# One core, attention and a soft mixture of experts: first-layer weights in longer runs and partly on another queue, a 512-wide second layer, and a new order of stages

## The chip, the core and the metric

The kernel runs on one core of one Trainium2 chip. The time is the device time of an execution in microseconds (us). Before the change, 8 executions took 182.0 us at the median, 181.5 to 182.68. One further execution was recorded by the hardware profiler; every view below is of that one.

## What is computed

The inputs are `q`, `k`, `v` of shape (8 batches, 8 heads, 576 positions, 64), `phi` (512 x 32), `w1` (8 experts, 512 x 1024) and `w2` (8 experts, 1024 x 512), all f32. Attention has a window of 32 positions, plain for heads 0 to 3 and with dilation 4 for heads 4 to 7. Its output, as 4,608 tokens of 512 features, goes through a soft mixture of experts with 4 slots an expert:

```python
scores = where(mask[h], q @ k.T / 8, -1e9);  x = softmax(scores) @ v      # x: (4608, 512)
logits = x @ phi
d = softmax over tokens of logits;   slot_input = (d.T @ x).reshape(8, 4, 512)
slot_out[e] = relu(slot_input[e] @ w1[e]) @ w2[e]
c = softmax over slots of logits;    out = c @ slot_out                   # (4608, 512)
```

Every expert's slots depend on all tokens, so the first layer can't start before attention has ended for the last batch, and no output can be stored before the second layer is done.

## The kernel before, in words

**A planner orders the work.** The program builds a list of operations, each with an engine, an assumed duration, a priority and its buffers. `Sched.run` then walks through time: of the operations that are ready on an engine at about the same time, the one with the lowest priority number goes first. Each engine executes its operations in the order so found, with a semaphore wait where an operation depends on another engine. The priority of a stage of half `i` is `i * PERIOD + OFFS[stage]`. It decides the order on an engine, not a start time.

**Attention** goes by 16 halves: batch `i // 2`, heads 0 to 3 or 4 to 7. For each, GpSimd (POOL) issues the loads of k, q and v (`load_half`, L328), which cast f32 to bf16 on the way into one of four staging buffers. VectorE (DVE) transposes them in 32 x 32 blocks (L455, L461), TensorE (PE) makes the scores with the mask added by an identity matmul (L475, L482, L492, L499), ScalarE (ACT) takes the exponential (L514), PE transposes v (L536) and ACT copies it out (L542), PE multiplies by v (L569, L593), and DVE divides (L576, L580, L601, L604). After the two halves of a batch, PE transposes x (L620, L626), ACT copies (L636, L639, L643), PE makes the logits (L659), ACT their exponential (L667), PE transposes that (L682), ACT copies it (L688), and PE and DVE add to the slot sums (L700, L708). In L626 and L700 a chunk of 128 features is a contiguous range.

**Loads** are all issued by POOL in one written order: the three loads of a half, then as many w1 pieces as `W_AFTER` says (two after half 1, one after most others), and after half 15 the last w1 piece and all of w2. A w1 piece (`w1_piece`, L338) is 256 rows, 1 MB of f32: partition p gets rows p and p + 128, two runs of 4 KB. A w2 piece (L345) is 1 MB in runs of 8 KB. The last two experts' w2 comes in slabs of half the columns (`w2_slab`, L352, runs of 1 KB), so that the left half of the output can be made while the right half's weights still load. Experts 5 to 7 of w2 use the space of the staging buffers. Some mask and identity tiles are built at the start on POOL (L381 to L411, selects at L388) and DVE (memsets from L400 to L424, L397, L402); POOL's loads of halves 2 and later stand behind its mask selects. `phi` is loaded by SP (L432) and converted by DVE (L437).

**The tail.** The first layer is 64 matmuls of 512 columns (L765) with a relu on ACT (L773) and a transpose (L783, L788). The second layer (`l2`, L801) is made for the left 256 columns and the right 256 columns apart, each in a PSUM bank of its own, 32 x 256 a matmul; ACT copies each result (L818). The output is 36 tiles of 128 tokens (L836), scaled on ACT (L845) and DVE (L848) in turn, and stored by SP (L856). The first three groups of 512 tokens (`NA = 3`) are stored in half rows, left and then right; groups 3 to 8 in full rows, two tiles (512 KB) a store.

## Time and profile before

| | |
|---|---|
| median of 8 executions | 182.0 us |
| profiled execution | 181.82 us |
| its span, first to last instruction | 180.0 us |
| PE, DVE, ACT, POOL busy | 126.2, 113.5, 104.3, 52.8 us |
| read from HBM, written | 61.93 MB, 9.44 MB |
| queue fed by POOL, queue fed by SP | 30.94 MB, 9.50 MB as written at the destination |
| k, q, v load: size, issue to landing | 288 KB each as written, 19.8 to 20.2 us |

In the views, "PEld" is TensorE's loading of weights, "SPq" and "POOLq" are instructions that issue transfers, and "a <- b" after an idle time names what ended it. "GB/s" counts the bytes that the transfers write: a load that casts f32 to bf16 reads twice as much. The "DMA share" is the mean busy share of 16 transfer engines by the durations of their packets; overlapping packets bring it over 1. "PEclk" is the granted share of TensorE's clock.

### The profile page before, as it was taken

The page shows a single profiled execution, that of the slowest core. Times are in us where ns is not written, and L with a number is a line of the kernel's source. Part 1 is how long each engine was busy: PE and PEld are TensorE (multiplying, and loading weights), DVE is VectorE, ACT ScalarE, POOL GpSimd, SP SyncE. Part 2 cuts the span into 40 slices and gives each one's busy share as a digit, 9 for nine tenths or more (in the row PEclk, how much of TensorE's full clock was granted, in tenths as well). Part 3 has the DMA queues.
Part 4 walks back from the last instruction along what each step waited for, and adds up shares of the span by engine and source line. Part 5 has one row for each costly group of instructions (what it writes and reads, how often), then busy time and mean ns, then how long its engine had stood idle before and what let it go on. Part 6 is the DMA issues. An engine that isn't in the chain of part 4 may idle for free.

```text
span 180.0 us, 5369 instructions
## 1 busy us (share of the span) xinstructions
PE 126.2 (70%) x2268; PEld 89.4 (50%) x2268; DVE 113.5 (63%) x211; ACT 104.3 (58%) x167; POOL 52.8 (29%) x99
## 2 busy tenths in 40 slices
PE   0027795989699799797898897795659766898000
PEld 0004474767467577476676675584434554442000
DVE  6898382957899798998879797835020103299200
ACT  0007366579778788869889788684324103399000
POOL 7679922223235244245860000740000000000000
PEclk9999996599999999999999999997556998799755
DMA  5999999999999999999999999999999999979998
GB/s 68 196 209 213 209 211 212 212 209 210 210 212 213 209 211 210 211 211 210 211 209 213 209 213 212 217 211 213 216 211 215 198 197 159 328 265 388 404 406 318
DMA packets 22727, 40.78 MB, mean 227 GB/s; under 512 B 2224, under 2 KB 9392, under 8 KB 22704
## 3 DMA queue, kind: packets, MB, share of 16 engines
q0 software_dynamic: 17184, 30.94, 93.0%
q1 hardware_dynamic: 5520, 9.50, 14.2%
q8 instruction: 18, 0.29, 0.6%
q14 instruction: 5, 0.04, 0.1%
HBM read 61.93 MB, written 9.44 MB: 396 GB/s over the span
## 4 chain that ended last, share of the span: by engine, by line
DMA 44%; PE 20%; DVE 15%; ACT 8%; issue 3%; POOL 1%; DVEq 0%; ACTq 0%
DMA ar<-in_v_dram 25%; DMA ar<-in_moe_w_dram 19%; PE ps L475 5%; ACT ar L514 5%; DVE ar L455 4%; DVE ar L848 4%; PE ps L836 3%; PE ps L801 2%; PE ps L482 2%; PE ps L536 2%; PE ps L569 2%; DVE ar L580 2%; DVE ar L415 2%; ACT ar L636 1%; PE ps L659 1%
## 5 line engine op out<-in xcount | busy, mean ns | idle before, releaser
L455 DVE STREAM_TRANSPOSE ar<-ar 128x576 uint32<-128x576 uint32 x40 | 48.1, 1244 | 2.4 <-DMA ar<-in_k_dram 1.8
L514 ACT ACTIVATE ar<-ps 128x1152 bf16<-128x1152 f32 (+1 forms) x32 | 38.1, 1192 | 13.9 <-PE ps L499 8.6
L475 PE MATMUL ps<-ar 128*128 128x320 bf16 (+1 forms) x128 | 24.1, 314 | 18.8 <-DVE ar L455 12.6
L542 ACT ACTIVATE ar<-ps 128x768 bf16<-128x768 bf16 x32 | 25.6, 831 | 2.8 <-PE ps L536 2.7
L580 DVE TENSOR_TENSOR ar<-ps,fs 96x768 bf16<-96x768 f32 (+1 forms) x32 | 26.3, 823 | 1.3
L475 PEld LDWEIGHTS ps<-ar 128*128 128x128 bf16 x128 | 11.0, 102 | 23.4 <-POOL ar L388 12.6
L848 DVE TENSOR_SCALAR ar<-ps,fs 128x256 f32<-128x256 f32 (+1 forms) x24 | 12.9, 611 | 12.7 <-PE ps L836 12.7
L569 PE MATMUL ps<-ar 128*128 128x65 bf16 x320 | 15.3, 199 | 6.6 <-ACT ar L514 3.3
L536 PE MATMUL ps<-ar 128*128 128x128 bf16 x192 | 17.8, 239 | 1.4 <-issue 0.5
L569 PEld LDWEIGHTS ps<-ar 128*128 128x128 bf16 x320 | 12.6, 101 | 9.0 <-ACT ar L514 5.2
L576 DVE RECIPROCAL fs<-ps 96x12 f32<-96x12 f32 (+1 forms) x32 | 6.1, 192 | 16.8 <-PE ps L569 16.7
L536 PEld LDWEIGHTS ps<-ar 128*128 128x128 bf16 x192 | 13.9, 122 | 3.2 <-issue 1.6
L328 POOL DMA_DIRECT2D ar<-in_k_dram x16 | 9.3, 582 | 20.7 <-DVE ar L455 11.6
L639 ACT ACTIVATE ar<-ps 128x1024 bf16<-128x1024 bf16 x8 | 8.2, 1022 | 7.6 <-PE ps L626 7.6
L345 POOL DMA_DIRECT2D ar<-in_moe_w_dram x12 | 6.4, 586 | 20.6 <-DVE fs L601 20.6
L328 POOL DMA_DIRECT2D ar<-in_v_dram x16 | 8.8, 551 | 12.2 <-DVE ar L455 7.5
L836 PE MATMUL ps<-ar 128*128 128x256 bf16 (+1 forms) x48 | 11.1, 356 | 1.8 <-ACT ar L818 1.0
L845 ACT ACTIVATE ar<-ps,fs 128x256 f32<-128x256 f32 (+1 forms) x24 | 11.5, 618 | 1.2 <-PE ps L836 1.2
L328 POOL DMA_DIRECT2D ar<-in_q_dram x16 | 8.8, 549 | 10.0 <-DVE fs L576 4.9
L338 POOL DMA_DIRECT2D ar<-in_moe_w_dram x16 | 11.7, 737 | 0.0
L659 PE MATMUL ps<-ar 128*128 128x288 bf16 x64 | 10.3, 306 | 1.9 <-ACT ar L643 1.9
L801 PE MATMUL ps<-ar 128*32 128x256 bf16 x128 | 8.8, 280 | 2.7 <-DMA ar<-in_moe_w_dram 2.3
(65 smaller groups left out, 179.3 us busy)
## 6 DMA issues: line engine op xcount, KB each, us to landing
ar<-in_moe_w_dram POOLq DMA_DIRECT2D x30, 512.0 KB, 26.3
out_dram<-ar SPq DMA_DIRECT2D x12, 512.0 KB, 5.0
ar<-in_k_dram POOLq DMA_DIRECT2D x16, 288.0 KB, 19.9
ar<-in_q_dram POOLq DMA_DIRECT2D x16, 288.0 KB, 19.8
ar<-in_v_dram POOLq DMA_DIRECT2D x16, 288.0 KB, 20.2
out_dram<-ar SPq DMA_DIRECT2D x12, 256.0 KB, 3.5
ar<-in_moe_w_dram POOLq DMA_DIRECT2D x4, 256.0 KB, 34.9
fs<-in_moe_phi_dram SPq DMA_DIRECT2D x1, 64.0 KB, 2.0
```

Source lines behind the costliest of these rows:

```text
L328: return pool.dma_start(a(o_stg + (s * 3 + j) * 1152, [[1, 1152]]), src[b, 4 * dl:4 * dl + 4].rearrange("h (p t) d -> (h p) (t d)", p=32))
L455: return dve.transpose(au(o_dst, [[1, 18], [18, 32]]), au(src, [[32, 18], [1, 32]]))
L475: pe.matmul(pf(h, 0, [[1, W]]), a(o_id, [[1, 128]]), a(msk, [[1, W]]), start=True, stop=False)
L514: eo = op(ACT, lambda P=P, W=W: act.activation(a(P, [[W, 4], [1, W]]), AP(ps, 0, [[4096, 128], [512, 4], [1, W]]), ACTF.Exp, scale=SCALE), ...
L536: last = pe.transpose(pb(bank.idx, bb * 256 + par * 32, [[64, 4], [1, 32]]), src, a(o_id, [[1, 128]]))
L542: op(ACT, lambda t=t, bank=bank: act.activation(a(o_vb[vs] + 3 * t * VBK, [[66, 12], [2, 32], [1, 2]]), pb(bank.idx, 0, [[64, 12], [1, 32] ...
L569: last = pe.matmul(pf(bank.idx + x, 65 * t, [[1, 65]]), w, a(VB + t * VBK + 66 * h, [[1, 65]]), start=True, stop=True)
L580: op(DVE, lambda hp=hp, bank=bank: dve.tensor_tensor(a(ox + 128 * hp, [[64, 2], [256, NT], [1, 64]], 0, rows), pf(bank.idx, 0, [[512, 2], ...
L659: last = pe.matmul(pf(bank.idx, 0, [[1, 288]]), a(o_phis + 128 * c, [[1, 128]]), a(o_xt[xt] + 576 * c + 288 * g, [[1, 288]]), start=(c == ...
L801: last = pe.matmul(pf(sobank[s].idx, 0, [[1, 256]], 32 * j, 32), a(o_htz + 1024 * g + 128 * c + 32 * j, [[1, 32]]), a(w2off(e) + DM * c + ...
L836: op(PE, lambda: pe.matmul(pf(bank.idx, 0, [[1, cw]]), a(o_et + 512 * G + j, [[4, 128]]), a(o_so + c0, [[1, cw]]), start=True, stop=True), ...
L848: op(DVE, lambda: dve.tensor_scalar(dst, src(), sca, None, op0=AluOp.mult), dvet(cw, True), prio + .1, reads=[bank, b_rinv], writes=wr, na ...
```

## The change

- The rows 0, 2, 4, ... 254 of the first expert's w1 (512 KB of f32) are loaded by SP as its first instruction, uncast, into space that w2 of expert 4 uses later; ACT converts them with a copy as its first instruction. POOL's first w1 piece loads the other 128 rows alone.
- In a w1 piece, partition p now gets rows 2p and 2p + 1: one run of 8 KB. So that the first layer's chunks fit, x is cut into chunks of even and odd features: `phi` is loaded in that order (runs of 256 bytes instead of 128), and L620, L626 and L700 read x with a step of two features.
- The second layer of experts 0 to 5 is made 512 columns wide into a bank of its own. Partitions 0 to 63 (slots of experts 0, 1, 4, 5) are copied by ACT to their place, partitions 64 to 127 by DVE to f32 scratch. Experts 6 and 7 are still made by halves, and a DVE add replaces ACT's copy of each half.
- Groups 3 to 8 are stored with one 1 MB store each, after four tiles.
- `PERIOD` and all stage offsets are other numbers. Together with the new parts they give another order on PE, ACT and DVE; POOL's order of loads is the same. At the start, DVE now does the first k transpose ahead of L397 and L402, and POOL has the k load of half 2 ahead of the last two mask selects. Towards the end of attention, ACT copies the v of half 15 (L542) right after the last exponential; before, copies of half 14's x (L636, L639, L643, L688) stood between.

```diff
-PERIOD = 6.9
+PERIOD = 13.0
-OFFS = dict(T=0.0, SC=0.6, EX=1.2, MK=2.2, TB=1.0, VE=1.8, PV=4.0, RC=4.4, NM=4.6,
-            XT=6.6, XE=7.0, LG=8.0, EXL=8.5, ET=9.0, EE=9.4, SI=9.8, SA=10.2)
+OFFS = dict(T=11.1, SC=0.6, EX=1.0, MK=13.2, TB=-8.2, VE=-1.3, PV=-27.6, RC=-28.0, NM=-27.1,
+            XT=-13.0, XE=1.8, LG=-37.3, EXL=16.9, ET=26.7, EE=14.5, SI=23.9, SA=8.8)
...
-    def w1_piece(e, hf):
+    def w1_piece(e, hf, r0=0, n=2):
         def fn():
             return pool.dma_start(
-                a(o_w1 + e * 4096 + hf * 2048, [[1024, 2], [1, 1024]]),
-                moe_w1[e, 256 * hf:256 * hf + 256, :].rearrange("(c p) f -> p c f", p=128))
+                a(o_w1 + e * 4096 + hf * 2048 + 1024 * r0, [[1, 1024 * n]]),
+                moe_w1[e, 256 * hf:256 * hf + 256, :].rearrange("(p two) f -> p (two f)", two=2)
+                [:, 1024 * r0:1024 * (r0 + n)])
...
-        wq += [w1_piece(e, 0), w1_piece(e, 1)]
+        wq += [w1_piece(e, 0, 1, 1) if e == 0 else w1_piece(e, 0), w1_piece(e, 1)]
...
+    op(SP, lambda: spq.dma_start(
+        af(w2off(4), [[1, 1024]]),
+        moe_w1[0, 0:256, :].rearrange("(p two) f -> p two f", two=2)[:, 0, :]), .1, -200.0,
+       kind="dma", nbytes=1 << 19, sem=sem("s_w1f"), writes=b_w2[4], name="w1f")
+    op(ACT, lambda: act.activation(a(o_w1, [[1, 1024]]), af(w2off(4), [[1, 1024]]), ACTF.Copy),
+       1.1, -200.0, reads=b_w2[4], writes=[b_w1[0]], name="w1c")
...
-        f(o_phst, [[32, 4], [1, 32]]),
-        moe_phi.rearrange("(c p) s -> p c s", p=128)), .1, 20.0,
+        f(o_phst, [[64, 2], [1, 64]]),
+        moe_phi.rearrange("(hf p two) s -> p hf (two s)", hf=2, two=2)), .1, 20.0,
...
-                                            a(ox + 256 * t + 128 * x, [[1, 128]], 0, 96),
+                                            a(ox + 256 * t + x, [[2, 128]], 0, 96),
...
-                                            a(ox + 256 * t + 128 * par, [[1, 128]]),
+                                            a(ox + 256 * t + par, [[2, 128]]),
...
-                                     a(o + 256 * t + 128 * par, [[1, 128]], 0, rows),
+                                     a(o + 256 * t + par, [[2, 128]], 0, rows),
...
+    l2((0, 1, 2, 3), 0, 0, 512)
+    l2((4, 5), 0, 0, 512)
+    op(ACT, lambda: act.activation(a(o_so, [[1, 512]], 0, 64), pf(sobank[0].idx, 0, [[1, 512]], 0, 64),
+                                   ACTF.Copy), actt(512), T1 + 10, reads=[sobank[0]], writes=b_so,
+       name="SOx")
+    op(DVE, lambda: dve.tensor_copy(af(o_sx, [[1, 512]], 64, 64), pf(sobank[0].idx, 0, [[1, 512]], 64, 64)),
+       dvet(512, True), T1 + 10, reads=[sobank[0]], writes=[b_sx, b_p[2]], name="SOy")
+    for x in (1, 2):
+        l2((6,), x, 256 * x - 256, 256, bufs=[b_w2[6][x - 1]])
+        for y in range(2):
+            l2((7,), x, 256 * x - 256, 256, range(4 * y, 4 * y + 4), [b_w2h[y][x - 1]])
+        op(DVE, lambda x=x: dve.tensor_tensor(
+            a(o_so + 256 * x - 256, [[1, 256]], 64, 64), pf(sobank[x].idx, 0, [[1, 256]], 64, 64),
+            af(o_sx + 512 * x - 512, [[1, 256]], 64, 64), AluOp.add), dvet(256, True),
+           T1 + 10 + 20 * x, reads=[sobank[x], b_sx], writes=[b_so[x - 1]], name=f"SO{x - 1}")
...
     for G in range(NA, 9):
-        for x in range(0, 4, 2):
-            for j in (x, x + 1):
-                out_tile(G, j, 0, 512, T2 + 10 + G + .25 * x)
-            store(G, 0, 512, T2 + 10 + G + .25 * x + .2, x, 2)
+        for j in range(4):
+            out_tile(G, j, 0, 512, T2 + 10 + G)
+        store(G, 0, 512, T2 + 10 + G + .5)
```

## The prediction

> **What bounds the kernel now.** I read the page's second part first, the span in 40 slices, because it shows at a glance whether an engine or the transfers are never idle.
>
> ```profile
> DMA  5999999999999999999999999999999999979998
> GB/s 68 196 209 213 209 211 212 212 209 210 210 212 213 209 211 210 211 211 210 211 209 213 209 213 212 217 211 213 216 211 215 198 197 159 328 265 388 404 406 318
> ...
> HBM read 61.93 MB, written 9.44 MB: 396 GB/s over the span
> ...
> DMA 44%; PE 20%; DVE 15%; ACT 8%; issue 3%; POOL 1%; DVEq 0%; ACTq 0%
> ```
>
> The DMA row is 9 everywhere but in the first slice, in one near 158 us and at the end. The GB/s row counts bytes written: loads read f32 and write bf16, so 211 GB/s written is 422 read. At that rate the reads take 61.93/0.422 = 147 us and the stores at 406 another 23 us: 170 of 180 us. So the transfers set the time, and only their holes or their rate can change it. Next I read the busy time of the engines by stretches, to size holes and rates (columns: PE, PEld, DVE, ACT, POOL busy, clock, DMA share, GB/s).
>
> ```profile
> 0.00:1.80 1.80, 0.00 (x0) 0.00 (x0) 0.65 (x2) 0.00 (x0) 0.76 (x5) 1.00 0.00 0
> 1.80:2.40 0.60, 0.00 (x0) 0.00 (x0) 0.60 (x1) 0.00 (x0) 0.60 (x2) 1.00 0.69 109
> 2.40:3.40 1.00, 0.00 (x0) 0.00 (x0) 0.72 (x2) 0.00 (x0) 1.00 (x3) 1.00 0.69 48
> 14.00:104.00 90.00, 75.89 (x1546) 57.14 (x1539) 72.26 (x128) 70.60 (x103) 36.85 (x65) 0.96 1.11 211
> 114.50:139.30 24.80, 18.45 (x314) 12.97 (x302) 7.10 (x20) 12.07 (x23) 4.74 (x7) 0.72 1.06 214
> 157.60:158.90 1.30, 1.21 (x11) 0.70 (x8) 1.30 (x4) 1.30 (x5) 0.00 (x0) 1.00 0.27 84
> 158.90:163.50 4.60, 4.18 (x17) 1.43 (x17) 4.60 (x9) 4.60 (x10) 0.00 (x0) 1.00 1.01 340
> 163.50:179.00 15.50, 2.69 (x9) 0.55 (x7) 4.37 (x7) 3.15 (x6) 0.00 (x0) 0.66 1.02 406
> ```
>
> The reader is to see three things. Until 3.4 us almost nothing moves: 48 KB in the last of these microseconds where 211 would be normal. The long mixed stretch (q, k, v in 2,304-byte and w1 in 2,048-byte packets as written) runs at 211, the stretch of w2 pieces (4,096 bytes) at 214. Stores of half rows (1,024-byte packets) run at 340, those of full rows (4,096) at 406. Last, the chain in order of time and the tail of the time line, for the slack of the engines.
>
> ```profile
> 86.29 25.27 DMA ar<-in_v_dram
> ...
> 116.11 33.71 DMA ar<-in_moe_w_dram
> ...
> 149.96 0.61 PE ps L801 x4
> ```
> ```profile
> 134.32 4.50 PE L765 MATMUL ps<-ar 128*32 128x512 bf16 x48 [0.79 <-DVE ar L752]
> ...
> 142.37 3.67 PE L801 MATMUL ps<-ar 128*32 128x256 bf16 x96 [0.37 <-DVE ar L788]
> ...
> 148.53 0.61 PE L801 MATMUL ps<-ar 128*32 128x256 bf16 x4 [1.23 <-DMA ar<-in_moe_w_dram]
> ```
>
> The engines wait for the last w2 slabs, not the slabs for the engines.
>
> **The change part by part.** The profiled execution took 181.82 us, 180.0 of it span; the sum is made against that, and as the median of 8 runs is 182.0, I subtract the same amount from the median.
>
> *First w1 rows on SP's queue.* The first 1 MB w1 piece loses half: 128 packets of 2 KB. Counting packets by size in stretches of 2 to 5 us between 8 and 150 us and solving for the engine time of each size gives 157 to 158 ns for 2,048 bytes and 309.5 to 310 for 4,096. So 128 x 158 / 16 engines = 1.26 us leave the busy queue. The replacement is 128 packets of 4 KB, f32 to f32; the nearest row is the full-row store (4,096 x 16 / 406 GB/s = 161 ns), 1.29 us. It is SP's first instruction, where the phi load now issues at 0.74 us and moves its first packet at 1.8; so it fills 1.8 to 3.1 us. What it can push aside there is 48 KB, 0.23 us of normal rate; I take 0.15. phi (before: 512 packets of 13 ns, 0.42 us, in an empty queue) now comes behind it, into the busy time, with half the packets: 0.21 by packets, 0.42 by bytes; 0.25, since short packets go by number. (Its reader on DVE, L437 at 9.91, is far off.) Net gain 1.26 - 0.15 - 0.25 = 0.86. Bounds: 1.26, and -0.28 if the queue gains no time at all (1.29 + 0.25 against 1.26). The Trainium skill speaks against this part (DMA: Bandwidth & Descriptors, Rules for kernel authors): issuing from several engines doesn't help bandwidth, since all use the same 16 engines; it saves only issue time. By that the gain is POOL's first issue at 1.24 less SP's at 0.74, 0.5 us, less phi: 0.25. The row 2.40:3.40 says the engines stand nearly empty just then, so I stay with 0.86.
>
> *w1 in 8 KB runs.* The other 15.5 pieces are 39 us of reading at 422. 1,920 pairs of 2 KB packets become 4 KB packets: 2 x 158 - 309.7 = 6 ns a pair, 1,920 x 6 / 16 = 0.7 us. Bounds from the rows 211 and 214: nothing, if only q, k and v are the slow ones; 1.3 us, if the whole 1.3% of 90 us is w1's (1.28, with the rest of its pieces outside). The packets' own durations (174 ns against 324) would say 24 ns a pair, 2.8 us, but they overlap (share 1.11 against 1.06), so I don't believe that. The skill (same page, Why small descriptors are slow) charges 32 bytes of metadata a descriptor: halving the descriptors saves 32 in 8,192, 0.4% of 39 us, 0.16 us. I take 0.6, near the packets, which are measured here.
>
> *Stores of full rows, 1 MB each instead of 512 KB.* 1,536 packets of 4 KB become 768 of 8 KB. From 340 and 406: 48.2 and 161.4 ns a packet, so 10.5 ns are fixed; 768 x 10.5 / 16 = 0.5. Packets of 8 KB are not in the trace as stores; bounds 0 (cut to 4 KB again) and 0.6; I take 0.45. The first of them now waits for four tiles instead of two, about 0.75 us more (L848 512 wide takes 744 ns, ACT's 754, side by side). The half-row stores ahead of it keep the queue busy to 163.5, it would be issued near 162.1: covered by some 0.7 us; without the cover up to 0.75 us are lost once.
>
> *Second layer 512 wide.* 96 matmuls of 256 before the slabs (3.67 us) become 48 of 512. It is hidden by the wait for the slabs (1.23 us idle at 148.53), so it gives nothing. On the path: ACT's copy L818 (384 ns) becomes a DVE add of 64x256, nearest row L604, 415 ns: 0.03 twice. DVE has nothing queued before the first add; the second stands behind six evictions that ended 2 us earlier. The two early moves of six experts' sums are ACT and DVE work of about 0.6 us at 142 to 148 us, both idle there.
>
> *Waits at the start.* ACT's first instruction now waits for the w1 rows (about 4.5 us) and converts them, about 1.1 us; ACT had nothing before 14.41. It also pulls the 1.28 us table load off the first exponential. On DVE the first transpose (1.17 us) goes ahead of the reduction and the two mask preparations L402, so POOL's mask selects wait for them until 11.3 instead of 10.15, and behind them stands POOL's load queue. POOL now does three selects (1.6 us) instead of seven before the next k load: issue near 13.0, as before (13.03). But there is less queued: 2.56 MB instead of 2.82 written, dry at 3.4 + 2.56/0.211 = 15.5 us. From issue to first packet the first load took 1.4 us: 14.4. Covered by 1 us; beyond that each microsecond costs one.
>
> *Stage order, even/odd features.* Weights are now read with a stride in L620, L626 and L700. L536 has such reads already, 88 ns each (6 in 0.53 us), contiguous L626 73 (10 in 0.73): at most 15 ns for 44 matmuls a batch, 0.7 us of PE in 13.4, where PE idles 2.1. Loads land about 20 us after issue, so transposes may come several microseconds later without emptying the queue. Taken at nothing.
>
> Sum: 0.86 + 0.6 + 0.45 - 0.05 = 1.86. Profiled 181.82 - 1.86 = 180.0; against the median 182.0, 180.1 us. The hole at 157.6 to 158.9 stays and moves forward: what is late next is still the last w2 slab and then the stores.
>
> **Rivals.** *Rate unchanged:* packets of 8 KB bring nothing in w1 or stores, because bytes set the rate; only the start gains. For it: 211 against 214 is little. Against: 340 against 406. 182.0 - 0.86 + 0.05 = 181.2; if the start also gives only the skill's 0.25, 181.8, no change that can be told. *Packets count fully:* 2.8 for w1: 182.0 - 0.86 - 2.8 - 0.5 = 177.8; against it, the share falls with packet size. *Engines late (slower):* the new order of stages lets attention slip, and the first layer becomes the bound. The slabs of the first half now end near 148.4. From the first layer's start to the end of its path PE needs 8.05 us to the second layer, then 2.6 to 3.7, 1.05 and 0.61: 12.3 to 13.4. So it must start by 135.0 to 136.1; it started at 134.32. Each later microsecond costs one, and past about 137.5 the kernel is slower than before. For it: DVE is busy 72 of 90 us in the mixed stretch, and PE 76. Against it: v of the last half lands 1.4 us earlier, and its V copies no longer stand behind other copies on ACT (they ended at 123.67). With a slip to 139: 183.5.
>
> **How the numbers follow.** Forecast 0.64 (179.0 to 181.0), rate unchanged 0.18 (half of it within the bound of no change), packets count fully 0.10, engines late 0.08. The range takes in the forecast, most of the rate case and the near end of the packet case: 178.5 to 181.7. About 0.3%, 0.55 us, is what a measurement can tell here from no change. Faster: 0.64 + 0.10 + 0.09 = 0.83; same 0.09 + 0.01 = 0.10; slower 0.07.
>
> **What would show it.** The first slices: over 150 GB/s between 2.4 and 3.4 us, and SP's queue first. The mixed stretch at 212 to 213. The last stretch at 412 or more. The last slab's matmuls of the first half near 148.5, PE still waiting for them, a hole near 156 of about the same length. Span near 178.2. It is wrong if the DMA share drops under 1 between 14 and 140 us, if the first layer starts after 136, or if the mixed stretch stays at 211.

## The result, and the profile after

The changed kernel takes 181.9 us at the median, 180.95 to 183.4; the kernel before beside it took 181.7. The ratio, which weighs all the executions and not the medians alone, is 1.0024, 95% interval 1.0007 to 1.0041: slower by 0.4 us, where 1.9 us less was forecast. (Executions that ran disturbed, over 1.5% above the fastest of their kernel, are left out here and below: five of the changed kernel, 184.3 to 184.9 us.) The times fall into two groups, 8 of 180.95 to 181.95 us and 7 of 182.69 to 183.4. The profiled execution took 182.98 us, with a span of 181.2, so the delays read below are those of the slower group; no profile shows the quicker one.

First the page of the changed kernel: slices of the span, bytes, and the shares of the chain.

```profile
DMA  5999999999999999999999999999999996999994
GB/s 139 203 211 211 215 208 212 216 210 210 215 209 211 215 208 214 212 210 212 214 211 210 212 212 216 211 218 210 214 213 212 195 196 89 311 326 412 421 418 199
...
HBM read 61.93 MB, written 9.44 MB: 394 GB/s over the span
...
DMA 45%; DVE 22%; PE 18%; ACT 4%; issue 2%; POOL 1%; DVEq 0%; POOLq 0%
```

The first slice moves twice as much as before (139 against 68) and the last full slices reach 421 against 406. But the hole stands in another place, in the slice from 149.5 to 154.0 us (89 GB/s), and the last slice is no longer full. Stretches, columns as in the prediction:

```profile
2.40:3.40 1.00, 0.00 (x0) 0.00 (x0) 0.72 (x2) 0.00 (x0) 1.00 (x3) 1.00 1.05 254
14.00:104.00 90.00, 77.22 (x1598) 57.67 (x1588) 72.83 (x129) 71.57 (x107) 34.27 (x66) 0.98 1.09 212
114.50:139.30 24.80, 17.70 (x319) 11.52 (x316) 6.19 (x18) 9.91 (x19) 4.10 (x6) 0.93 1.06 214
143.60:147.20 3.60, 3.59 (x16) 1.16 (x16) 0.00 (x0) 0.00 (x0) 0.00 (x0) 0.50 1.45 197
150.00:154.40 4.40, 3.64 (x21) 2.08 (x22) 1.86 (x5) 1.55 (x5) 0.00 (x0) 0.82 0.52 70
163.70:178.50 14.80, 2.72 (x9) 0.57 (x8) 4.42 (x7) 3.20 (x6) 0.00 (x0) 0.67 1.02 421
179.00:180.40 1.40, 0.00 (x0) 0.00 (x0) 0.00 (x0) 0.00 (x0) 0.00 (x0) 0.50 0.06 23
```

The start, the mixed stretch and the stores came as forecast. The last two rows did not. From 150 to 154.4 the transfers are half idle: the last w2 packet ends at 153.70, 1.2 us earlier than before (154.88), but the first store moves its first packet at 154.39, 1.2 us later (153.19). And from 179.0 to 180.4 the DMA share is 0.06: one engine of 16 (1/16 = 0.0625) works alone, while the others end at 178.9.

The tail of TensorE's time line (start, length, then in brackets the idle time and what ended it), and DVE's two lines there:

```profile
127.04 4.46 PE L775 MATMUL ps<-ar 128*32 128x512 bf16 x48 [0.73 <-DVE ar L762]
...
135.16 1.91 PE L813 MATMUL ps<-ar 128*32 128x512 bf16 x32 [0.47 <-DVE ar L798]
143.59 3.60 PE L813 MATMUL ps<-ar 128*32 128x512 bf16 x16 [6.52 <-DMA ar<-in_moe_w_dram]
148.07 3.86 PE L813 MATMUL ps<-ar 128*32 128x256 bf16 x16 [0.88 <-DVE ar L829]
152.54 1.87 PE L854 MATMUL ps<-ar 128*128 128x256 bf16 x12 [0.61 <-DVE ar L835]
```
```profile
147.23 0.69 DVE L829 COPY ar<-ps 64x512 f32<-64x512 f32 x1 [12.28 <-PE ps L813]
151.97 0.43 DVE L835 TENSOR_TENSOR ar<-ps,ar 64x256 bf16<-64x256 f32 x1 [4.05 <-PE ps L813]
```

Read it downwards. The first layer starts 7.3 us earlier (134.32 before). So TensorE has done experts 0 to 3 by 137.1 and waits 6.5 us for the w2 of experts 4 and 5. In that idle time its clock falls: the records show half clock from 141.36 to 151.60 (0.50 in the row 143.60:147.20). At half clock the 16 matmuls of 4 and 5 take 3.60 us; at full clock, in a kernel shown below, 1.90. Then it waits 0.88 us for DVE's move of the wide sum (L829): the planner gave the first half's sum (`soA`) the very PSUM bank that the wide sum (`soX`) leaves. (A bank is one of the places that matmuls write their sums to.) Then experts 6 and 7 follow, still at half clock, and the left half is done at 151.94, 3.3 us after its last slab landed (148.63). Before, this was 0.75 us (149.82 to 150.57). The chain says the same; it no longer passes through the slabs but through the bank:

```profile
113.34 30.01 DMA ar<-in_moe_w_dram
...
143.59 3.61 PE ps L813 x16
147.20 0.02 issue
147.23 0.71 DVE ar L829
...
151.09 0.86 PE ps L813 x4
151.94 0.02 issue
151.97 0.44 DVE ar L835
```

### The profile page after: what moved, and what is told of

Read it like the earlier page. It is cut to its first block, busy times and chain, and to the rows that moved or that the text cites. A ratio compares the mean times of both kernels' runs of the same rounds, so it can differ in the third digit from the quotient of the medians.

```text
span 181.2 us, 5283 instructions
## 1 busy us (share of the span) xinstructions
PE 125.9 (69%) x2220; PEld 85.9 (47%) x2220; DVE 113.9 (63%) x214; ACT 105.5 (58%) x167; POOL 49.5 (27%) x99
## 4 chain that ended last, share of the span: by engine, by line
DMA 45%; DVE 22%; PE 18%; ACT 4%; issue 2%; POOL 1%; DVEq 0%; POOLq 0%
DMA ar<-in_k_dram 28%; DMA ar<-in_moe_w_dram 17%; DVE ar L465 7%; PE ps L813 5%; DVE ar L866 5%; PE ps L485 3%; DVE ar L590 2%; ACT ar L524 2%; PE ps L546 2%; PE ps L579 2%; DVE ar L425 2%; PE ps L492 1%; ACT ar L646 1%; PE ps L854 1%; DVE ar L471 1%
## 5 line engine op out<-in xcount | busy, mean ns | idle before, releaser
L465 DVE STREAM_TRANSPOSE ar<-ar 128x576 uint32<-128x576 uint32 x40 | 48.7, 1241 | 6.6 <-DMA ar<-in_k_dram 6.6
L552 ACT ACTIVATE ar<-ps 128x768 bf16<-128x768 bf16 x32 | 25.1, 819 | 2.6 <-PE ps L546 2.5
L485 PEld LDWEIGHTS ps<-ar 128*128 128x128 bf16 x128 | 10.9, 102 | 20.5 <-POOL ar L398 12.6
L546 PE MATMUL ps<-ar 128*128 128x128 bf16 x192 | 16.2, 234 | 3.0 <-DVE ar L590 2.7
L813 PE MATMUL ps<-ar 128*32 128x512 bf16 (+1 forms) x80 | 11.5, 412 | 8.2 <-DMA ar<-in_moe_w_dram 6.5
L579 PEld LDWEIGHTS ps<-ar 128*128 128x128 bf16 x320 | 12.6, 100 | 6.1 <-issue 4.3
L546 PEld LDWEIGHTS ps<-ar 128*128 128x128 bf16 x192 | 12.8, 120 | 4.3 <-DVE ar L590 2.2
L347 POOL DMA_DIRECT2D ar<-in_moe_w_dram x12 | 6.4, 581 | 20.6 <-DVE ar L465 20.6
L813 PEld LDWEIGHTS ps<-ar 128*32 128x32 bf16 x80 | 5.2, 111 | 14.2 <-issue 11.3
L854 PE MATMUL ps<-ar 128*128 128x256 bf16 (+1 forms) x48 | 10.5, 334 | 1.8 <-DVE ar L835 1.1
L646 ACT ACTIVATE ar<-ps 128x576 bf16<-128x576 bf16 x16 | 9.5, 648 | 1.8 <-PE ps L630 1.6
L669 PE MATMUL ps<-ar 128*128 128x288 bf16 x64 | 9.2, 287 | 1.0 <-ACT ar L653 1.0
```

The source lines that it names most:

```text
L465: return dve.transpose(au(o_dst, [[1, 18], [18, 32]]), au(src, [[32, 18], [1, 32]]))
L485: pe.matmul(pf(h, 0, [[1, W]]), a(o_id, [[1, 128]]), a(msk, [[1, W]]), start=True, stop=False)
L546: last = pe.transpose(pb(bank.idx, bb * 256 + par * 32, [[64, 4], [1, 32]]), src, a(o_id, [[1, 128]]))
L552: op(ACT, lambda t=t, bank=bank: act.activation(a(o_vb[vs] + 3 * t * VBK, [[66, 12], [2, 32], [1, 2]]), pb(bank.idx, 0, [[64, 12], [1, 32] ...
L579: last = pe.matmul(pf(bank.idx + x, 65 * t, [[1, 65]]), w, a(VB + t * VBK + 66 * h, [[1, 65]]), start=True, stop=True)
L813: last = pe.matmul(pf(sobank[x].idx, 0, [[1, n]], 32 * j, 32), a(o_htz + 1024 * g + 128 * c + 32 * j, [[1, 32]]), a(w2off(e) + DM * c + co ...
```

## The experiments

My theory: the transfers gained what was forecast, and the wide second layer gives it back, through the bank and the half clock. Rivals: 1 MB stores are bad at the end, the new order of stages is, or a late engine has a cause of its own.

### The bank, the clock and the old second layer

**a_bank.** Expert 6's first operation also claims the wide sum's bank, so that this bank is not free yet when the next is given out. The order on every engine is that of the changed kernel.

```diff
-           rmw=[sobank[x]], name=f"L2{es[0]}{x}{cs[0]}")
+           rmw=[sobank[x]], name=f"L2{es[0]}{x}{cs[0]}",
+           banks=[sobank[0]] if es == (6,) and x == 1 else ())
```

> The changed kernel with one thing undone: the second layer of experts 6 and 7 no longer takes over the PSUM bank of the 512-wide sum, so TensorE does not wait for VectorE's move of that sum (0.88 us before its 16 matmuls at 148.07). Theory (TensorE is late in the tail, at half clock after its long wait for w2): the left half's sum is ready about 0.9 us sooner (151.1 instead of 152.0), the hole in the transfers before the first store shrinks by as much, the time falls by 0.5 to 0.9 us. Rival 1 (the 1 MB stores and one late transfer engine set the end): no change, within 0.3. Rival 2 (the transfers of the loads set everything): no change.

Measured: 180.87 us, 0.9951 times before (0.9934 to 0.9969). Repeated later on another chip as c_bank (below): 0.9971. So the bank that is used again costs the changed kernel 1.0 to 1.3 us (0.53% to 0.73% of 181.7), somewhat more than expected. TensorE's lines of a_bank:

```profile
143.72 4.97 PE L813 MATMUL ps<-ar 128*32 128x512 bf16 x28 [6.64 <-DMA ar<-in_moe_w_dram]
148.89 0.60 PE L813 MATMUL ps<-ar 128*32 128x256 bf16 x4 [0.20 <-DMA ar<-in_moe_w_dram]
150.09 1.87 PE L855 MATMUL ps<-ar 128*128 128x256 bf16 x12 [0.61 <-DVE ar L836]
```

The idle time is the same, 6.64 us, and so is the half clock (141.24 to 148.07). But work goes on without a gap, the last four matmuls wait for their slab again, and the left half is done at 149.49, 2.4 us earlier. The executions of a_bank lie within 0.5 us and the 22 of c_bank within 0.8, in one group.

**a_warm.** 28 more matmuls of 512 columns, on data already there and into a bank that nobody reads, between experts 0 to 3 and experts 4 and 5; they fill the wait, so that the clock stays up. The shifted order also gives `soA` another bank.

```diff
     l2((0, 1, 2, 3), 0, 0, 512)
+    wb = Bank("warm")
...
+    op(PE, warm_fn, pet(28, 512), T1 + 6, reads=[b_htz, b_w1[0]], writes=[wb], name="warm")
     l2((4, 5), 0, 0, 512)
```

> The changed kernel with 28 matmuls of 512 columns added on TensorE between the 512-wide sums of experts 0 to 3 and those of 4 and 5, into a bank that nobody reads; they fill the wait for w2 from 137 to 143 us. The bank order also drops the 0.88 us wait for VectorE. Theory (the clock fell to half because TensorE stood idle 6.5 us, and at half clock it ends the left half 2 us after its last slab): the clock stays at 1.0 from 131 to 151, experts 4 and 5 take 1.9 us instead of 3.6, experts 6 and 7 follow the slabs, the left half's sum is ready near 150.0 instead of 152.0, and the time is 1.2 to 1.9 us under the changed kernel's. Rival 1 (stores and a late transfer engine): within 0.3 of the changed kernel. Rival 2 (only the bank wait): as the kernel with the bank alone freed, 0.5 to 0.9 less.

Measured: 180.66 us, 0.9938 (0.9915 to 0.996). Its clock is full from 132.6 to 166.7, and the left half is done at 149.53: no earlier than in a_bank. So the half clock alone does not delay the left half: the slabs hide it. A later kernel (a_pad100, below) shows the opposite half. In its profiled execution the bank wait stays, the clock is full, and the last four matmuls again wait for their slab:

```profile
143.75 1.90 PE L822 MATMUL ps<-ar 128*32 128x512 bf16 x16 [2.49 <-DMA ar<-in_moe_w_dram]
146.49 1.78 PE L822 MATMUL ps<-ar 128*32 128x256 bf16 x12 [0.83 <-DVE ar L838]
148.96 0.61 PE L822 MATMUL ps<-ar 128*32 128x256 bf16 x4 [0.69 <-DMA ar<-in_moe_w_dram]
```

Only together do the two reach the path.

**a_oldl2.** The changed kernel with the second layer of before: two sums of 256 columns, each with its own bank, and ACT's copies.

```diff
-    sobank = [Bank("soX"), Bank("soA"), Bank("soB")]
+    sobank = [Bank("soA"), Bank("soB")]
...
+    for es_ in ((0, 1, 2, 3), (4, 5), (6,)):
+        for s in range(2):
+            l2(es_, s)
```

> The changed kernel with the second layer of the kernel before (two halves of 256 columns, ACT copies). Theory (half clock): experts 4 and 5 at half clock take 3.6 us again, then 6 and 7 without the wait for VectorE: like the kernel with the bank freed, 0.5 to 0.9 us under the changed kernel. Rival (the 512-wide form itself costs the time, by its add and moves): back at the kernel before less the gain of the loads, 1.5 us or more under the changed kernel.

Measured: 179.8 us, 0.9904 (0.9883 to 0.9926), the fastest version, ahead of both kernels; its repeat c_oldl2 gave 179.65, 0.9913. Here too TensorE waits (5.11 us) and the clock falls (0.5 from 143.1 to 146.55), and still the matmuls of the last slabs have to wait for them:

```profile
144.00 3.59 PE L812 MATMUL ps<-ar 128*32 128x256 bf16 x40 [5.11 <-DMA ar<-in_moe_w_dram]
147.84 0.60 PE L812 MATMUL ps<-ar 128*32 128x256 bf16 x4 [0.25 <-DMA ar<-in_moe_w_dram]
149.17 0.60 PE L812 MATMUL ps<-ar 128*32 128x256 bf16 x4 [0.73 <-DMA ar<-in_moe_w_dram]
150.33 2.12 PE L847 MATMUL ps<-ar 128*128 128x256 bf16 x12 [0.56 <-ACT ar L829]
```

The old second layer is 0.9 us (a_oldl2 against a_bank) to 1.1 us (c_oldl2 against c_bank) faster than the wide one with its bank freed. So the bank and the clock are not all: by number this is the rival's outcome, in which the wide form costs 1.5 us or more. The last part of the experiments goes after this rest.

### The parts on the transfers, one by one

**a_oldst.** The changed kernel with stores of 512 KB for groups 3 to 8.

```diff
-        for j in range(4):
-            out_tile(G, j, 0, 512, T2 + 10 + G)
-        store(G, 0, 512, T2 + 10 + G + .5)
+        for x in range(0, 4, 2):
+            for j in (x, x + 1):
+                out_tile(G, j, 0, 512, T2 + 10 + G + .25 * x)
+            store(G, 0, 512, T2 + 10 + G + .25 * x + .2, x, 2)
```

> The changed kernel with the 512 KB stores of the kernel before for groups 3 to 8. Theory (TensorE late, half clock): the stores' rate falls from 421 back to 406 GB/s, 0.5 us more than the changed kernel. Rival (1 MB stores leave one transfer engine 1.7 us behind at the end): the engines end together again and the time falls by about 1 us.

Measured: 182.35 us, 1.0053 (1.0024 to 1.0082). Against 1.0024 with 1 MB stores these are 0.5 us more, near the 0.45 that I took, though the intervals overlap. One transfer engine ends late here too (179.80 against 178.6), so 1 MB stores are not its cause.

**b_start.** The kernel before, with w1 rows 0 to 127 on SP's queue and ACT's conversion.

```diff
-        wq += [w1_piece(e, 0), w1_piece(e, 1)]
+        wq += [w1_half() if e == 0 else w1_piece(e, 0), w1_piece(e, 1)]
...
+    op(SP, lambda: spq.dma_start(
+        af(w2off(4), [[1, 1024]]), moe_w1[0, 0:128, :]), .1, -200.0,
+       kind="dma", nbytes=1 << 19, sem=sem("s_w1f"), writes=b_w2[4], name="w1f")
...
```

> The kernel before with the first 128 rows of w1 on SP's queue (4 KB runs, in the old order of rows) and ACT's conversion, nothing else. By the prediction 0.86 us faster. By the trace of the changed kernel, where k of half 0 starts 1.33 us later and v of half 2 lands 0.67 us sooner: 0.5 to 0.7 us faster. Rival (same transfer engines, only issue time is gained): 0 to 0.25.

Measured: 180.61 against 180.93 us, 0.9986 (0.9968 to 1.0003): 0.25 us, and the interval takes in no gain at all.

**b_8k.** The kernel before, with w1 in runs of 8 KB and the even and odd features that belong to it.

```diff
-                a(o_w1 + e * 4096 + hf * 2048, [[1024, 2], [1, 1024]]),
-                moe_w1[e, 256 * hf:256 * hf + 256, :].rearrange("(c p) f -> p c f", p=128))
+                a(o_w1 + e * 4096 + hf * 2048, [[1, 2048]]),
+                moe_w1[e, 256 * hf:256 * hf + 256, :].rearrange("(p two) f -> p (two f)", two=2))
...
```

> The kernel before with w1 in 8 KB runs, even and odd features and phi to match, nothing else. By the prediction 0.6 us faster. By the landings in the changed kernel (0.38 us gained between half 2 and half 15): 0.3 to 0.5. Rival (bytes set the rate, or the strided weights cost): none, or slower.

Measured: 180.34 against 180.93 us, 0.9969 (0.9954 to 0.9983): 0.56 us, where 0.6 was the sum.

### Width and order together

Four kernels fill the table of second layer and order. "Loads, stores" are the start, the w1 runs and the 1 MB stores.

**b_l2** is the kernel before with the new second layer (its planner finds a free bank for `soA`). **a_offs** and **a_oldl2offs** are the changed kernel with the old `PERIOD` and `OFFS`, the second also with the old second layer. **b_offs** is the kernel before with the new ones. One number of the planner goes with the loads and not with the order: the time at which it takes the load queue to start (`qfree`), 3.3 us in the kernels from before and 0.6 in the changed ones. So the same offsets need not give the same order in both.

```diff
-PERIOD = 6.9
+PERIOD = 13.0
...
-OFFS = dict(T=0.0, SC=0.6, EX=1.2, MK=2.2, TB=1.0, VE=1.8, PV=4.0, RC=4.4, NM=4.6,
-            XT=6.6, XE=7.0, LG=8.0, EXL=8.5, ET=9.0, EE=9.4, SI=9.8, SA=10.2)
+OFFS = dict(T=11.1, SC=0.6, EX=1.0, MK=13.2, TB=-8.2, VE=-1.3, PV=-27.6, RC=-28.0, NM=-27.1,
+            XT=-13.0, XE=1.8, LG=-37.3, EXL=16.9, ET=26.7, EE=14.5, SI=23.9, SA=8.8)
```

> The kernel before with the 512-wide second layer alone. Its planner gives the first half's sum (soA) a bank that is free, so no matmul waits for the two moves. If the cost of the new second layer is the bank that is used again (0.88 us of waiting) and the idle time ahead of the sums of experts 4 and 5, which this old order hardly has (its first layer starts near 134.3): within 0.3% of before, 0.999 to 1.002 times, first store near 153.2. If the wide sums themselves cost, because 16 matmuls of 512 columns stand just ahead of the last slabs: 0.5 us slower or more, 1.003 and over, with the last slab's matmuls of the left half later than 149.7.

> The kernel after with the old PERIOD and stage offsets: all of the change but the order of stages. Here too the planner gives the first half's sum a free bank. If the order is what lets the two sums meet in one bank and makes TensorE idle before the sums of experts 4 and 5, this gets the start, the w1 runs and the stores without their price: 0.25 + 0.56 + 0.5 = 1.3 us under before, 0.993 times. If the new order also brings something of its own (the difference between the parts' sum and the version with the old second layer, 0.4 us): 0.995 to 0.996. If the wide sums cost by themselves: 0.997 or more.

> The kernel after with the old second layer and the old order: only the start, the 8 KB w1 runs and the 1 MB stores are left. If the parts add up: 1.3 us under before, 0.993 times. If the order is worth nothing or the parts gain more together: 0.990, as with the old second layer and the new order.

> The kernel before with the new PERIOD and stage offsets alone. The first layer should start near 127 instead of 134.3, TensorE should idle before the second layer's experts 4 and 5 and its clock fall, but the old second layer has its banks to itself, so the end is set by the slabs as before. If the order is worth nothing: within 0.3% of before. If it gives the 0.4 us that the parts' sum leaves over: 0.998. If the idle time and the half clock cost by themselves: 1.003 or more.

Measured, as ratios to before with their intervals:

| | second layer 256 wide | 512 wide |
|---|---|---|
| old loads, stores; old order | 1 | 1.0053 (1.0032 to 1.0073), b_l2 |
| old loads, stores; new order | 1.0036 (1.0018 to 1.0055), b_offs | not run |
| new loads, stores; old order | 1.0044 (1.0027 to 1.0061), a_oldl2offs | 0.9994 (0.9974 to 1.0015), a_offs |
| new loads, stores; new order | 0.9904 (0.9883 to 0.9926), a_oldl2 | 1.0024 (1.0007 to 1.0041), the change |

a_oldl2offs fits none of its branches. The other three fall by number into the branch in which the wide sums cost by themselves (b_l2, a_offs) or the idle time does (b_offs). But in b_l2 the last slab's matmuls of the left half come at 148.90 and not after 149.7, and in b_offs the first layer comes later, not near 127, so that there is no idle time. The sum of parts fails: with the new loads and stores the width costs 2.2 us beside the new order and gains 0.9 beside the old. Some of this is not width or order: in b_l2, a_oldl2offs, a_offs and the changed kernel one transfer engine ends 0.7 to 1.4 us late, in the other three none does (last part below). a_oldl2offs:

```profile
136.57 4.68 PE L775 MATMUL ps<-ar 128*32 128x512 bf16 x48 [0.99 <-DVE ar L762]
...
145.15 5.46 PE L812 MATMUL ps<-ar 128*32 128x256 bf16 x112 [0.78 <-DVE ar L798]
151.60 1.05 PE L812 MATMUL ps<-ar 128*32 128x256 bf16 x8 [0.99 <-DMA ar<-in_moe_w_dram]
152.57 2.13 PE L847 MATMUL ps<-ar 128*128 128x256 bf16 x12
```

With the old order the first layer starts at 136.57, the second at 145.15, and its 112 matmuls run on without a wait for the slabs: the left half is done at 150.61, 0.8 us later than in a_oldl2 (149.77). Worse, the planner now has the first matmuls of the right half (expert 6, the eight at 151.60) ahead of the first output. They wait 0.99 us for their slab and take 1.05, and the first output starts at 152.57, where a_oldl2 has it at 150.33. So of the 2.2 us by which its first output lags, 0.8 are the late first layer and 1.4 the place of eight matmuls.

b_offs shows the late first layer alone, with the right half in its old place (its lines, then the first output of the kernel before):

```profile
137.71 4.59 PE L765 MATMUL ps<-ar 128*32 128x512 bf16 x48 [0.79 <-DVE ar L752]
...
145.85 5.54 PE L801 MATMUL ps<-ar 128*32 128x256 bf16 x112 [0.36 <-DVE ar L788]
151.96 0.93 PE L836 MATMUL ps<-ar 128*128 128x256 bf16 x7 [0.56 <-ACT ar L818]
```
```profile
151.12 2.10 PE L836 MATMUL ps<-ar 128*128 128x256 bf16 x10 [0.56 <-ACT ar L818]
```

No wait for a slab is left, the first output starts at 151.96 instead of 151.12, and the kernel is 0.65 us slower (0.36%). This is the rival "engines late", past its limit of 135.0 to 136.1. In a_offs the first layer is late too (136.10), but its next 60 matmuls (48 of 512 columns, 12 of 256) take 4.09 us from 144.17 on, the last four wait for their slab, and the left half is done at 149.55. So the wide sum and the earlier first layer cure the same trouble; where the first layer is early, the width has nothing to gain and keeps its price. In b_offs the new numbers make the first layer later, in the changed kernel earlier. Which of the offsets, `qfree` or the new loads does it was not taken apart.

TensorE's granted clock between 127 and 134 us is 0.50 in the kernel before and in a_oldl2offs and 0.76 in the changed kernel, so the end of attention runs partly at half clock where the first layer is late; whether this makes it late or comes with it was not tried.

b_l2 lost 1 us though its first store moves early (152.85). Its profile shows one engine that ends at 179.62, the others at 178.4; this leads to the last question.

### The engine that ends late

In the records of packets, one transfer engine ends late in some kernels and not in others. What goes with it is where the last 16 KB packet of TensorE's instructions falls (queue "instruction", 0.88 to 1.33 us long; a fetch, below), against the last pause of the stores. A pause is here a stretch of 0.15 us or more with under eight packets under way; the hole of the kernel before, 157.85 to 158.95, is one.

| kernel | last fetch | lag of the last engine |
|---|---|---|
| before, b_8k, b_start, b_pad110, b_offs, a_warm, a_bankpad100, a_oldl2, c_oldl2 | 152.1 to 158.7, a pause of 0.2 to 1.1 us follows | up to 0.2 us |
| a_oldl2offs, a_offs | 158.7 and 159.8, a pause of 0.15 and of 0.35 us follows | 0.7 and 0.8 |
| a_oldl2pad88, c_bank, a_bank, b_l2, a_oldst, the change, a_pad100 | 159.2 to 168.6, no pause follows | 0.9 to 1.7 |

A reading that fits: a fetch puts one engine behind, a pause lets that engine catch up, and after the last pause nothing does. But the lengths of pause and lag do not match one to one, and these are 18 profiles of one execution each, so the part of the pause is argued.

In the changed kernel, from 163.5 to 165.5, the full-row stores share the engines with one such packet, which takes 3.0% of 16 engines in 2 us, 0.96 us of one:

```profile
q1 hardware_dynamic: 211, 0.84, 106.7%
q8 instruction: 1, 0.02, 3.0%
```

To move the fetch, matmuls of one column are put at TensorE's start; no result uses them. All other instructions keep their order on every engine, though their times can shift.

```diff
+        padb = Bank("pad")
+        def pad_fn():
+            for _ in range(100):
+                last = pe.matmul(pf(padb.idx, 0, [[1, 1]], 0, 32), a(o_vb[0], [[1, 32]]),
+                                 a(o_vb[0], [[1, 1]]), start=True, stop=True)
+            return last
+        op(PE, pad_fn, pet(100, 1), D0, reads=[b_vb[0][0]], writes=[padb], name="pad")
```

**a_bankpad100** is a_bank with 100 of these, **b_pad110** the kernel before with 110.

> The changed kernel with the bank freed, and 100 tiny matmuls (one column, into a bank that nobody reads) at TensorE's start, where it waits for the first data; they move the 16 KB blocks of TensorE's instruction fetch forward in time, the one at 162.0 us to before 148. Theory (a fetch in the stretch of stores holds one transfer engine for a microsecond, and that engine ends 1.3 us after the others): the stores end together, and the time falls by 0.9 to 1.3 us against the kernel with the bank freed, to 179.6 to 180.0. Rival (the 512-wide form costs its microsecond otherwise, the fetch nothing): no change against it, 180.9.

> The kernel before with 110 such tiny matmuls at TensorE's start. The fetch at 157.7 us (where the transfers stand still anyway) moves to before 145, and the next one comes to about 162, into the stores. Theory (fetch in the stores): one transfer engine ends about 1 us late, 0.7 to 1.2 us slower than before. Rival: no change within 0.3.

Measured: a_bankpad100 179.86 us, 0.9947 (0.9928 to 0.9967). Its fetch moved from 162.0 to 152.1 and its engines end evenly (177.27; the last one of a_bank at 178.37), but by ratio it gains nothing on a_bank (0.9951) and at most 0.4 us on c_bank (0.9971): the rival's outcome. Its median is 0.8 to 1.0 us under theirs, but it ran on another chip, and the kernel before differs by up to 0.8 us between chips (180.93 to 181.69). So it leaves open what the fetch costs the wide form. b_pad110: 181.64 us, 1.0029 (1.0014 to 1.0044), 0.5 us slower; its fetch stayed at 158.09 (157.68 before), so it does not test a fetch behind the last pause.

The two kernels show something else, though: a fetch just ahead of a pause is not free either. In b_pad110 SP takes 1.56 us to issue the store of 158.11, during the fetch, where most take 0.4 to 0.7, and a second pause opens from 159.6 to 160.25. In a_warm, whose fetch falls at 156.95, the store of 156.85 takes 1.56 us too; from 158 to 159 the DMA share is 0.20 where a_bank has 1.01, and the bulk of the stores ends at 177.9 instead of 176.9. This would explain that a_warm ends evenly and is still only 0.2 us faster than a_bank and 0.9 slower than a_oldl2 on the same chip. That the fetch holds up the issue is read from these profiles and was not tried.

Four more kernels went to one chip:

> The kernel after with 100 matmuls of one column more at the start of TensorE's work, on data that nobody reads; the order on every engine is the same. They shift TensorE's instruction stream, so that the last 16 KB fetch falls some 100 matmuls from the end instead of 7: near 153 us instead of 164. The wait for the bank stays. If the late fetch is what makes one transfer engine end 1.5 us behind the others: an even end and 1.0 to 1.3 us under after, 0.995 to 0.997 times before. If the late engine has another cause or the fetch costs as much wherever it falls: as after, 1.002.

> The kernel after with the old second layer, the fastest so far, with 88 matmuls of one column more at TensorE's start; the order is the same. Its last fetch, 47 matmuls from the end at 152.81, should move ahead of the tail, and the next should come into reach some 7 matmuls from the end, near 161 to 163, among the full-row stores. If a fetch there makes one engine late: that engine ends over 1 us behind the others, and the time is 1 us over c_oldl2, 0.995 to 0.997 times before. If not: as c_oldl2, 0.990.

> The kernel after with the old second layer once more, to stand on the same chip as the two with padding: 0.990 times before, an even end, the last fetch near 153.

> The kernel after with the wide sum's bank held once more, on the same chip as the others: 0.995 times before, one engine over 1 us behind the others, the last fetch near 162. If its lag behind c_oldl2 was the chip's: 0.990.

Measured: c_oldl2 179.65 us, 0.9913 (0.9888 to 0.9939), last fetch 153.7, even end. a_oldl2pad88 180.67 us, 0.997 (0.9952 to 0.9988), last fetch 159.16, one engine 0.9 us late: 1.0 us slower by 88 matmuls that do nothing. c_bank 180.66 us, 0.9971 (0.9957 to 0.9985), fetch 161.48, 1.3 us late: with a fetch among the last stores in both, the wide form with its bank freed and the old one take the same time. The end of c_oldl2 and then of a_oldl2pad88:

```profile
177.10:177.30 0.20, 0.00 (x0) 0.00 (x0) 0.00 (x0) 0.00 (x0) 0.00 (x0) 0.50 0.02 0
177.30:177.90 0.60, 0.00 (x0) 0.00 (x0) 0.00 (x0) 0.00 (x0) 0.00 (x0) 0.50 0.00 0
```
```profile
177.10:177.30 0.20, 0.00 (x0) 0.00 (x0) 0.00 (x0) 0.00 (x0) 0.00 (x0) 0.50 0.00 0
177.30:177.90 0.60, 0.00 (x0) 0.00 (x0) 0.00 (x0) 0.00 (x0) 0.00 (x0) 0.50 0.06 27
```

In the second, share 0.06 again: one engine alone. a_pad100 missed: 181.15 us, 1.0014 (0.9989 to 1.0038). Its padding brought another fetch into reach, at 168.61, and one engine ends 1.7 us late; also its first layer slipped to 130.50, and its wait for w2 shrank to 2.49 us. Its executions fall into two groups like those of the changed kernel, 11 of 180.0 to 180.9 us and 11 of 181.4 to 182.6; what parts them no profile shows. So the fetch among the last stores costs about 1 us in the one pair that differs in nothing else and ran on one chip (c_oldl2, a_oldl2pad88); what the changed kernel itself would take without it was not measured.

## Why the prediction was wrong

**The step that failed** is "Second layer 512 wide": "hidden by the wait for the slabs (1.23 us idle at 148.53), so it gives nothing", with the two moves as work of ACT and DVE, "both idle there". The engines were idle, but the move stands between two uses of one PSUM bank, so TensorE waits behind it; I did not look at which bank the next sum would get. And the cover of 1.23 us was taken from the old order at full clock. In the new order TensorE has been idle for 6.5 us, its clock is half, and the 3.6 us of experts 4 and 5 eat the cover. In the profiles either alone is hidden (a_pad100, a_bank); both together have the left half done 3.3 us after its last slab. Price: 1.0024 less 0.9951 of 181.7, 1.3 us, or 1.0 by c_bank. The spread says it too: the changed kernel's executions differ by 2.45 us, c_bank's 22 by 0.8.

The Trainium skill (TensorE: Matmul & The Clock Gate, Part 1) says that the clock halves after an idle window of about 3.4 us, that a busy one of that length restores it, and that the windows run free of the kernel. The trace agrees in kind: idle from 137.1 to 143.6, half clock from 141.36. But half clock lasts 8.0 us after this wait in the changed kernel, whose work has a gap, 4.4 after the same in a_bank (143.7 to 148.07) and 2.6 in a_oldl2. With the rule I should have let the 16 wide matmuls cost double; I did not ask for TensorE's clock there at all.

**Not in the sum at all:** one transfer engine that ends late. Which kernel it hits goes with where a fetch of TensorE's instructions falls; nothing in the profile of before, whose last fetch fell next to its hole, showed a price. If it costs the changed kernel the 1.0 us that it cost the old second layer, then with 1.0 to 1.3 for the bank it makes up 2.0 to 2.3 of the 2.3 us between the forecast -1.9 and the result +0.4; both terms are uncertain by some 0.3 to 0.5, by their intervals. The bank's share is shown. The fetch's share is argued from another form of the kernel; a_bankpad100, the trial on the wide form, does not confirm it.

**Also wrong:** "Stage order", "Taken at nothing." Beside the old second layer the new order is worth 1.0044 less 0.9904, 2.5 us: with the old order the new loads meet a late first layer (0.8 us) and a right half ahead of the first output (1.4). Beside the wide one it gains nothing (0.9994 with the old order, 1.0024 with the new): there it also brings the long wait and the half clock. Up to 0.8 us of either difference can be the late engine's. I worked out the limit (135.0 to 136.1), but looked for a loss only, and not at what the second layer does when the first comes 7 us early. The hole, which "stays and moves forward", closed where the second layer kept up (a_oldl2 has only a dip near 154.5).

**Right:** the transfers set the time once the engines keep up. Size by size: w1 runs 0.6, measured 0.56; stores 0.45, measured 0.5, within the noise; the first w1 rows 0.86, measured 0.25 alone (-0.05 to 0.58), though the last packet of half 2's v came 0.67 us earlier in the changed kernel (21.31 against 21.98). That term was too large: POOL's first k load moved its first packet at 3.96 us instead of 2.63, so more was pushed aside than the 0.15 taken. The 0.25 that I worked out from the Trainium skill (DMA: Bandwidth & Descriptors, Rules for kernel authors) and set aside is within the interval. With the old second layer, these parts and the order give 0.9904, 1.7 us less than before, close to the 1.9 forecast. In part this is luck: the parts on the transfers alone, in the old order, are slower than before (a_oldl2offs), so the order taken at nothing was needed for it.

**The signs named ahead:** the rate at 2.4 to 3.4 us (254), the mixed stretch (212) and the last one (421) came true; the last slab's matmuls with TensorE waiting, a hole near 156 and a span of 178.2 did not. The first two are the second layer's; the span, 181.2, is also the late engine's. None of the three signs of being wrong appeared (the first layer started at 127.04, the mixed stretch ran at 212 with share 1.09): they watch attention and the long stretch of loads, and the loss came behind both.

## What to carry to other kernels

Before a step is called hidden, ask which buffer the next step gets and at which clock it will run after the wait that hides it; an engine that is made ready earlier waits longer and can come back slower (here after 6.5 us, at half clock). Where a planner gives out banks and places, read its result after each edit: one bank used again cost 1.0 to 1.3 us here, eight matmuls in the wrong place held the first output up by 1.4. Two cures for the same lateness do not add up. If the end of a kernel is a full queue of stores on all engines, look in its last microsecond for a share of 1/16, and for an instruction fetch after the last pause before it. Where the executions of a kernel fall into two groups, ask which of them the profile shows.

## What the runs showed of the hardware

- TensorE, idle for 6.5 us (137.1 to 143.6), was granted half its clock from 141.36 on. 16 matmuls of 512 columns then took 3.60 us instead of 1.90 (a_pad100, granted clock 1.00), and half clock lasted 8.0, 4.4 and 2.6 us after such a wait in the changed kernel, a_bank and a_oldl2.
- In 9 of 18 profiles one of 16 transfer engines ends 0.7 to 1.7 us after the others, and in each of these an instruction packet of 16 KB, 0.88 to 1.33 us long, falls among the last stores. From 179.0 to 180.4 us of the changed kernel the DMA share is 0.06, about 1/16: no other engine takes over the rest.
- With a transfer of 512 KB on SP's queue at the start, POOL's k load moved its first packet 1.3 us later (3.96 against 2.63), though in the kernel before only 48 GB/s moved there.
- 88 matmuls without use at the start of a kernel, with the order on every engine unchanged, made it 1.0 us slower (179.65 to 180.67); its last fetch moved from 153.7 to 159.2.
